# Decode attention with a gated MLP: the last weight rows on 24 and 25 lanes, the output sum in 160-column halves

## The chip, the cores and the metric

The kernel runs on one core of one Trainium2 chip. The metric is the device time of one execution in microseconds; lower is better. A profiled execution gives the trace that is read here. Times in the text count from the start of the profiled span.

## The reference

One token for each of 4 batch rows, width 640, all inputs and the output in bf16:

```python
xn = layernorm(x)                                  # [4, 1, 640], no scale or shift
# A: attention over a cache, 32 heads of 128, 4096 cached rows a head
q = (xn @ wq)                                      # [640, 4096], split in 32 heads
p = softmax(q . k_cache / sqrt(128))               # k_cache, v_cache [4, 32, 4096, 128]
A = (p . v_cache).reshape(4, 1, 4096) @ wo         # wo [4096, 640]
# B: gated MLP; the sequence is 1, so w_sp is [1, 1] and b_sp is [1]
z = gelu_tanh(xn @ w_in)                           # w_in [640, 1728]
z1, z2 = z[..., :864], layernorm(z[..., 864:])
B = (z1 * (w_sp * z2 + b_sp)) @ w_out              # w_out [864, 640]
out = x + A + B
```

K and V are 134 MB each; the weights w_q, w_o, w_in and w_out come to 13.8 MB.

## The kernel before

The work is cut into 16 units (`NU`), each with 8 heads of one batch row. A unit's K is 8 MB and its V is 8 MB. A load has 128 partitions with 64 KB in a row each. K lies in a ring of seven quarter slots (`k_ring`), V in one buffer (`v_all`).

For each quarter of a unit's K, `product` (L537, DVE) multiplies K by the broadcast query, `fold_half` (L543, DVE) adds the two halves of each row, and `sums` (L555, PE) adds the rest by matmuls with an identity into PSUM; `row_sums` (L569, DVE) ends the scores. `head_max`, `exps` and `by_head` make the softmax weights (ACT, DVE), `weighted` (L631, PE) multiplies them with V, and every four units `group_turn` and `group_proj` (L678 to L699) apply w_o. The output is summed in one PSUM tile, `out_ps`: partitions 0 to 3 hold the sum for columns 0 to 319, partitions 32 to 35 the one for columns 320 to 639 (`out_sum`). It starts with x, added by a matmul with the identity (L373).

All large loads are issued by SP's queue in the order of the list `loads`; `pump` issues the next one when its buffers are no longer in `busy`. The list starts with the first half of unit 0's K in two loads, then `load_w` (w_in, and w_out's first 768 rows), the second half of that K, `load_w_few` (w_out's last 96 rows) and unit 1's K; after these V and K alternate. w_q is loaded before all of them (L118). V's buffer holds w_q, w_in and w_out's first 640 rows at the start, so unit 0's V waits for the MLP's matmuls. The order of instructions on PE, DVE, ACT and SP is the order in which they are written in the `manual_schedule` block.

w_out's 864 rows are placed by `W_OUT`, with lanes, rows a lane and number of transfers: 128 x 5 in one, 128 x 1 in one, and 12 x 8 in four transfers of three lanes each (each lane then is one run of 8 rows, 10240 bytes).

```python
W_OUT = ((P, 5, 1), (P, 1, 1), (12, 8, 4))
```

The MLP is the generator `gmlp`; its steps run between the first two quarters of unit 0. w_sp and b_sp, 2 bytes each, are loaded by ACT after the first query has been copied (L735, L736). x is one transfer of four rows, issued by ACT (L101).

At the end `group_proj` adds the last eight heads, for each head columns 0 to 319 and then 320 to 639. w_o's last group comes in six transfers, the last head in two halves of 320 columns. ACT copies the whole of `out_ps` (L823), and ACT and SP write one half of the output each (L824, L825).

## Time and profile before

| what | value |
|---|---|
| time, median of 3 runs | 662.07 us (661.95 to 662.16) |
| time of the profiled execution | 662.09 us |
| its span, first to last instruction | 660.2 us |
| mean granted TensorE clock | 0.692 |
| busy: PE, DVE, ACT, POOL | 317.0, 522.6, 29.9, 10.1 us |
| moved by DMA | 282.55 MB, 428 GB/s over the span |
| share of 16 DMA engines' span on SP's and ACT's load queues | 99.1% and 0.0% |

The profiled execution's time is the span and 1.9 us outside it. Busy times of different engines overlap. The DMA share is the mean over the core's 16 DMA engines; a 128-row load gives each of them eight rows. "SPq" and "ACTq" are the issues of transfers on SP's and ACT's queue, not the transfers themselves.

### The profile page before, as it was taken

What the parts mean: (1) busy time and instruction counts of PE and PEld (TensorE: products, weight loads), DVE (VectorE), ACT (ScalarE), POOL (GpSimd) and SP (SyncE); (2) the same over time, 40 slices, a digit from 0 to 9 for tenths busy, and PEclk for the clock granted to TensorE, in tenths of its full rate; (3) what the DMA queues carried; (4) which work ended last, traced back from release to release, by engine and by line L of the source; (5) the groups of instructions that cost most, each with busy time, mean ns of one, the idle gap of its engine ahead of it and who ended that gap; (6) DMA issues with size and microseconds to landing.
All of it is one profiled execution on the core that took longest, in us unless ns stands there. A gap on an engine that the chain in (4) does not pass through costs nothing.

```text
span 660.2 us, 4777 instructions
## 1 busy us (share of the span) xinstructions
PE 317.0 (48%) x2083; PEld 136.3 (21%) x2083; DVE 522.6 (79%) x276; ACT 29.9 (5%) x73; POOL 10.1 (2%) x20
## 2 busy tenths in 40 slices
PE   0574372526427363452636336263452534737367
PEld 0231121212213121120212112121120211212124
DVE  1767978959597795969959598695969969999950
ACT  0020000000000000000000000000000000000000
POOL 2300000000000000000000000000000000000000
PEclk9757676766767676585767768676685867676785
DMA  9999999999999999999999999999999999999997
GB/s 369 433 461 434 417 441 434 433 437 438 421 445 426 437 430 441 437 422 433 434 441 441 418 437 441 430 441 421 434 441 437 426 421 445 422 427 436 449 409 284
DMA packets 8232, 282.55 MB, mean 428 GB/s; under 512 B 892, under 2 KB 2184, under 8 KB 2568
## 3 DMA queue, kind: packets, MB, share of 16 engines
q1 hardware_dynamic: 8192, 282.25, 99.1%
q8 instruction: 16, 0.26, 0.1%
q10 hardware_dynamic: 20, 0.01, 0.0%
q14 instruction: 4, 0.03, 0.0%
HBM read 282.24 MB, written 0.01 MB: 428 GB/s over the span
## 4 chain that ended last, share of the span: by engine, by line
DMA 62%; DVE 28%; PE 8%; issue 1%; ACT 0%; DVEq 0%
DMA k_ring<-in_A_k_cache_dram 53%; DVE k_ring L537 14%; DVE k_ring L543 7%; PE s_ps L555 6%; DMA v_all<-in_A_v_cache_dram 4%; DMA k_ring<-in_A_wo_dram 3%; DVE s_sb L569 3%; DMA v_all<-in_A_wq_dram 2%; DVE p_m L607 1%; DVE m L578 1%; PE q_ps L303 1%; PE pv L631 1%; PE out_ps L699 1%; DVE p_m L678 1%; DVE mf L580 1%
## 5 line engine op out<-in xcount | busy, mean ns | idle before, releaser
L537 DVE TENSOR_TENSOR k_ring<-k_ring,qbc 128x8192 bf16<-128x8192 bf16 x64 | 282.9, 4420 | 88.5 <-DMA k_ring<-in_A_k_cache_dram 87.9
L555 PE MATMUL s_ps<-k_ring,ident 128*128 128x512 bf16 x512 | 202.2, 566 | 313.8 <-DVE k_ring L543 313.7
L555 PEld LDWEIGHTS <-ident 128*128 128x128 bf16 x512 | 64.0, 130 | 430.0 <-issue 245.4
L543 DVE TENSOR_TENSOR k_ring<-k_ring 128x4096 bf16<-128x4096 bf16 x64 | 145.9, 2280 | 1.1
L631 PE MATMUL pv<-v_all,p_m 128*32 128x512 bf16 x960 | 62.5, 419 | 0.0
L569 DVE TENSOR_REDUCE s_sb<-s_ps 128x128 f32<-128x1024 f32 x32 | 39.0, 1218 | 3.7 <-PE s_ps L555 3.7
L607 DVE TENSOR_TENSOR p_m<-p_c,own 128x2048 bf16<-128x2048 bf16 x16 | 36.6, 2285 | 0.7 <-ACT p_c L596 0.7
L631 PEld LDWEIGHTS <-p_m 128*32 128x32 bf16 x992 | 26.6, 106 | 42.5 <-issue 23.3
L596 ACT ACTIVATE p_c<-s_sb,nm 128x256 bf16<-128x256 f32 x16 | 8.1, 508 | 342.9 <-DVE nm L588 342.9
L662 PEld LDWEIGHTS o_ps<-o_rows,pick 128*128 128x128 f32 x96 | 20.4, 294 | 4.3 <-issue 3.3
L662 PE MATMUL o_ps<-o_rows,pick 128*128 128x128 f32 x96 | 19.1, 367 | 0.0
L643 ACT COPY o_rows<-pv 128x512 f32<-128x512 f32 x16 | 9.4, 586 | 165.7 <-PE pv L631 165.7
L311 DVE TENSOR_SCALAR q_rows<-q_ps 128x512 bf16<-128x512 f32 x2 | 1.4, 692 | 12.8 <-PE q_ps L303 12.8
L817 DVE TENSOR_TENSOR o_n_last<-o_last,rden_all 128x32 bf16<-128x32 f32 x1 | 0.2, 192 | 12.2 <-PE o_last L809 12.2
L303 PE MATMUL q_ps<-v_all,xnT 128*32 128x512 bf16 x40 | 4.5, 630 | 9.3 <-DMA v_all<-in_A_wq_dram 9.3
L527 ACT CAST qbc<-qbc_ps 128x128 bf16<-128x128 f32 x16 | 4.3, 266 | 97.6 <-PE qbc_ps L519 97.6
L578 DVE TENSOR_REDUCE m<-s_sb 128x1 f32<-128x256 f32 x16 | 6.7, 420 | 0.5
L519 PE MATMUL qbc_ps<-q_rows,of_row 128*128 128x128 bf16 x32 | 6.0, 276 | 0.6 <-DVE q_rows L311 0.6
L519 PEld LDWEIGHTS <-of_row 128*128 128x128 bf16 x32 | 4.1, 132 | 8.1 <-issue 7.4
L716 PE MATMUL o_last<-hot,o_rows 128*128 128x8 f32 x32 | 4.9, 279 | 0.7 <-ACT o_rows L643 0.7
L716 PEld LDWEIGHTS o_last<-hot,o_rows 128*128 128x128 f32 x32 | 4.8, 226 | 1.8 <-ACT o_rows L643 1.6
L699 PE MATMUL out_ps<-k_ring,p_m 128*4 128x320 bf16 x48 | 4.0, 309 | 2.1 <-DVE p_m L691 2.1
(87 smaller groups left out, 81.4 us busy)
## 6 DMA issues: line engine op xcount, KB each, us to landing
k_ring<-in_A_k_cache_dram SPq DMA_DIRECT2D x5, 4096.0 KB, 27.2
v_all<-in_A_v_cache_dram SPq DMA_DIRECT2D x2, 4096.0 KB, 28.2
v_all<-in_A_wq_dram SPq DMA_DIRECT2D x1, 5120.0 KB, 15.4
k_ring<-in_A_k_cache_dram SPq DMA_DIRECT2D x2, 2048.0 KB
k_ring<-in_A_v_cache_dram SPq DMA_DIRECT2D x1, 4096.0 KB
k_ring<-in_A_wo_dram SPq DMA_DIRECT2D x3, 1280.0 KB, 20.6
v_all<-in_B_w_in_dram SPq DMA_DIRECT2D x1, 2160.0 KB
k_ring<-in_A_v_cache_dram SPq DMA_DIRECT2D x1, 2048.0 KB
```

What stands on the lines that cost most here:

```text
L303: nc.tensor.matmul(out=q_ps[k * QD : (k + 1) * QD], lhsT=xnT[:, c, :], rhs=wq_v[:, c, k, e], start=(c == 0), stop=(c == DC - 1),)
L519: nc.tensor.matmul(out=qb_ps[:], lhsT=of_row[:, e, b].rearrange("p k f l -> p (k f l)"), rhs=q_rows[e][:, hg, :], start=(e == 0), stop=(e ...
L537: nc.vector.tensor_tensor(out=t, in0=t, in1=qbcs[u][:, None, :].to_broadcast([P, HC, Dh]), op=ALU.mult)
L543: nc.vector.tensor_tensor(out=t[:, :, 0:HD2], in0=t[:, :, 0:HD2], in1=t[:, :, HD2:Dh], op=ALU.add)
L555: nc.tensor.matmul(out=s, lhsT=ident[:], rhs=t[:, :, g * RW : (g + 1) * RW], start=(g == 0), stop=(g == m - 1),)
L569: nc.vector.tensor_reduce(out=scores[u][:].rearrange("p (r c) -> p r c", r=NK)[:, lo : hi + 1 : hi - lo], in_=sums_ps.pop(n // 2)[:], axis ...
L578: nc.vector.tensor_reduce(out=m1[:], in_=scores[u][:], axis=AX.X, op=ALU.max)
L607: nc.vector.tensor_tensor(out=p_m[:, u % 2], in0=p_c.pop(u)[:].rearrange("p (g c) -> p g c", c=CB)[:, :, :, None].to_broadcast([P, NG, CB, HT]
L631: nc.tensor.matmul(out=pvs[u][cg * QD : (cg + 1) * QD, :], lhsT=p_m[:, u % 2, g0 + n].rearrange("p c h -> p (c h)"), rhs=v_at[:, n * CB : ...
L662: nc.tensor.matmul(out=gr[hg][:], lhsT=pick[:, c, Bsz - 1 - b : P + Bsz - 1 - b], rhs=o[:, c, :], start=(b == 0 and c == 0), stop=(b == Bs ...
L699: nc.tensor.matmul(out=out_sum(half), lhsT=o, rhs=wo_sb[:, n, half * NOH : (half + 1) * NOH], start=False, stop=(hg == HG - 1 and n == HT ...
L716: nc.tensor.matmul(out=o_last[0][:, :, :, u % Bsz], lhsT=o[:, c, :], rhs=hot[:, c, :].rearrange("p (k e) -> p k e", e=PAR), start=(c == 0) ...
```

## The change

- w_out's rows 640 to 863 are placed on 24 lanes with one row each and on 25 lanes with eight rows each. On the 25 lanes a lane's eight rows follow each other in w_out, one run of 10240 bytes. They are loaded in small transfers: before the second half of unit 0's K ("wide") three for the 24 lanes, one of five lanes and half of one lane; after it ("few") two of five lanes, three of three lanes and the other half of that lane.
- x is loaded in four transfers of one row. w_sp and b_sp are loaded right after it, at the start.
- The two sums in `out_ps` hold alternate blocks of 160 columns (0 to 159 with 320 to 479, and 160 to 319 with 480 to 639). In the last head the first blocks of both are added first, then the second blocks. The last copy is made in two halves of 160 columns, by DVE and ACT. Each output transfer has two pieces of 160 columns a row.
- In `gmlp`, the factors of GELU and layer norm are folded into fewer DVE instructions, the mean comes from a matmul with a column of 1/864, and b_sp is carried through the broadcast and added in the last step.

The diff, cut to its core:

```diff
@@ -59,14 +59,18 @@
     RW = 8
     QW = HC * Dh
     RING = 2 * NK - 1
-    W_OUT = ((P, 5, 1), (P, 1, 1), (12, 8, 4))
+    W_OUT = (
+        (P, 5, True, (("wide", 0, 128, 1),)),
+        (24, 1, True, (("wide", 0, 12, 1), ("wide", 12, 8, 1), ("wide", 20, 4, 1))),
+        (25, 8, True, (("wide", 1, 5, 4), ("few", 2, 5, 4), ("few", 7, 5, 4), ("few", 0, 3, 4), ("few", 3, 3, 9), ("few", 16, 3, 4), ("half", 22, 1, 1))),
+    )
...
@@ -98,7 +102,13 @@
 
     ring = places.tile([P, RING, QW], BF16, name="k_ring")
     x_bf = ring[0:Bsz, 1, 0:D]
-    nc.scalar.dma_start(out=x_bf, in_=A_x.flatten_outer_dims())
+    x_rows = A_x.flatten_outer_dims()
+    for b0, b1 in ((0, 1), (1, 2), (2, 3), (3, 4)):
+        nc.scalar.dma_start(out=x_bf[b0:b1], in_=x_rows[b0:b1])
+    wsp_bf = const.tile([1, 1], BF16)
+    bsp_bf = const.tile([1, 1], BF16)
+    nc.scalar.dma_start(out=wsp_bf[:], in_=B_w_sp[0:1, 0:1])
+    nc.scalar.dma_start(out=bsp_bf[:], in_=B_b_sp[0:1].rearrange("(a b) -> a b", a=1))
     v_all = places.tile([P, NK * QW], BF16, name="v_all")
 
     wq_sb = v_all[:, 0 : DC * HD].rearrange("p (c n) -> p c n", c=DC)
@@ -107,35 +117,42 @@
 
     at_v = up(DC * (HD + F))
     w_parts, f0, at_p = [], 0, 0
...
-    def load_part(part):
-        w, f0, n, r, t = part
-        rows = B_w_out[f0 : f0 + n * r].rearrange("(p k) n -> p k n", k=r)
-        for l in range(t):
-            nc.sync.dma_start(out=w[l:n:t], in_=rows[l:n:t])
+    def load_part(part, on):
+        w, f0, n, r, near, cuts = part
+        rows = B_w_out[f0 : f0 + n * r].rearrange(
+            "(p k) n -> p k n" if near else "(k p) n -> p k n", k=r
+        )
+        for kind, l, m, step in cuts:
+            if kind == on:
+                end = l + (m - 1) * step + 1
+                nc.sync.dma_start(out=w[l:end:step], in_=rows[l:end:step])
+            if kind == "half":
+                part_r = slice(0, r // 2) if on == "wide" else slice(r // 2, r)
+                nc.sync.dma_start(out=w[l : l + m, part_r], in_=rows[l : l + m, part_r])
 
     def load_w():
         nc.sync.dma_start(out=w_in_sb, in_=B_w_in.rearrange("(p c) n -> p c n", c=DC))
         for part in w_parts:
-            if part[4] == 1:
-                load_part(part)
+            load_part(part, "wide")
 
     def load_w_few():
         for part in w_parts:
-            if part[4] > 1:
-                load_part(part)
+            load_part(part, "few")
 
     w_rows = [
-        (w[:, i], f0 + i, n, r) for w, f0, n, r, _ in w_parts for i in range(r)
+        (w[:, i], f0 + i * (1 if near else n), n, r if near else 1)
+        for w, f0, n, r, near, _ in w_parts
+        for i in range(r)
     ]
 
     def run_of(cache, u):
@@ -251,6 +268,9 @@
     nc.gpsimd.memset(eps_tile[:], eps)
     ones_sq = const.tile([P, P], FP32)
     nc.gpsimd.memset(ones_sq[:], 1.0)
+
+    inv_fh = const.tile([P, 1], FP32)
+    nc.gpsimd.memset(inv_fh[:], 1.0 / float(Fh))
 
     NACC = 2
     row_den = [const.tile([P, Bsz], FP32, name=f"rd{n}") for n in range(NACC)]
...
@@ -366,14 +384,20 @@
     out_ps = ps_out.tile([P, NOH], FP32)
     OG = 32
 
-    def out_sum(half):
-        return out_ps[OG * half : OG * half + Bsz, :]
+    NS = 2
+    NP = NOH // NS
+
+    def out_sum(g):
+        return out_ps[OG * g : OG * g + Bsz, :].rearrange("b (s n) -> b s n", s=NS)
+
+    def columns(w, g):
+        return w.rearrange("p (s g n) -> p g s n", s=NS, n=NP)[:, g]
 
     for half in range(2):
         nc.tensor.matmul(
-            out=out_ps[OG * half : OG * half + OG, :],
+            out=out_ps[OG * half : OG * half + OG, :].rearrange("b (s n) -> b s n", s=NS),
             lhsT=ident[:Bsz, :OG],
-            rhs=x_bf[:, half * NOH : (half + 1) * NOH],
+            rhs=columns(x_bf, half),
             start=True,
             stop=False,
         )
@@ -384,11 +408,11 @@
     gm["gz"] = work.tile([P, 3, NFC, Bsz], FP32, name="gz")
     nc.gpsimd.memset(gm["zz"][:], 0.0)
     gm["st"] = work.tile([1, 5 * Bsz], FP32, name="st")
-    gm["ac"] = work.tile([1, 2 * Bsz], FP32, name="ac")
+    gm["ac"] = work.tile([1, 2 * Bsz + 1], FP32, name="ac")
     gm["yT"] = work.tile([P, NFC, Bsz], BF16, name="yT")
 
     by_lanes = []
...
@@ -411,29 +435,33 @@
         yield
         k0 = 0
         for n, ks in by_lanes:
-            nc.vector.tensor_copy(
-                out=zz[0:n, :, k0 : k0 + ks, :], in_=zT[0:n, :, k0 : k0 + ks, :]
+            nc.vector.tensor_scalar(
+                out=zz[0:n, :, k0 : k0 + ks, :],
+                in0=zT[0:n, :, k0 : k0 + ks, :],
+                scalar1=0.5,
+                scalar2=None,
+                op0=ALU.mult,
             )
             k0 += ks
-        nc.vector.tensor_tensor(out=gw[:], in0=zz[:], in1=zz[:], op=ALU.mult)
-        nc.vector.tensor_scalar(
-            out=gw[:], in0=gw[:], scalar1=0.044715, scalar2=1.0, op0=ALU.mult, op1=ALU.add
-        )
-        nc.vector.tensor_tensor(out=gw[:], in0=gw[:], in1=zz[:], op=ALU.mult)
+        nc.vector.scalar_tensor_tensor(
+            out=gw[:], in0=zz[:], scalar=4 * 0.044715, in1=zz[:], op0=ALU.mult, op1=ALU.mult
+        )
+        nc.vector.scalar_tensor_tensor(
+            out=gw[:], in0=gw[:], scalar=1.0, in1=zz[:], op0=ALU.add, op1=ALU.mult
+        )
         nc.scalar.activation(
-            out=gt[:], in_=gw[:], func=ACT.Tanh, scale=math.sqrt(2.0 / math.pi)
+            out=gt[:], in_=gw[:], func=ACT.Tanh, scale=2 * math.sqrt(2.0 / math.pi)
         )
         yield
-        nc.vector.tensor_scalar(
-            out=gt[:], in0=gt[:], scalar1=1.0, scalar2=0.5, op0=ALU.add, op1=ALU.mult
-        )
-        nc.vector.tensor_tensor(out=gz[:, 0:2], in0=zz[:], in1=gt[:], op=ALU.mult)
+        nc.vector.scalar_tensor_tensor(
+            out=gz[:, 0:2], in0=gt[:], scalar=1.0, in1=zz[:], op0=ALU.add, op1=ALU.mult
+        )
         sq = gz[:, 2, :, :]
         nc.vector.tensor_tensor(out=sq, in0=gz[:, 1, :, :], in1=gz[:, 1, :, :], op=ALU.mult)
 
         s_ps = ps_m.tile([1, 2, NFC, Bsz], FP32, tag="m", name="ln_ps")
         nc.tensor.matmul(
-            out=s_ps[:], lhsT=ones_sq[:, 0:1], rhs=gz[:, 1:3], start=True, stop=True
+            out=s_ps[:], lhsT=inv_fh[:], rhs=gz[:, 1:3], start=True, stop=True
         )
         yield
         st, ac = gm["st"], gm["ac"]
@@ -448,13 +476,6 @@
             axis=AX.X,
             op=ALU.add,
         )
-        nc.vector.tensor_scalar(
-            out=st[:, 0 : 2 * Bsz],
-            in0=st[:, 0 : 2 * Bsz],
-            scalar1=1.0 / float(Fh),
-            scalar2=None,
-            op0=ALU.mult,
-        )
         nc.vector.tensor_tensor(out=tmp_t, in0=mean_t, in1=mean_t, op=ALU.mult)
         nc.vector.tensor_tensor(out=var_t, in0=ex2_t, in1=tmp_t, op=ALU.subtract)
         nc.scalar.activation(
@@ -462,27 +483,25 @@
         )
         wsp_t = work.tile([1, 1], FP32, name="wsp_t")
         nc.gpsimd.tensor_copy(out=wsp_t[:], in_=wsp_bf[:])
-        bsp_t = work.tile([1, 1], FP32, name="bsp_t")
-        nc.gpsimd.tensor_copy(out=bsp_t[:], in_=bsp_bf[:])
+        nc.gpsimd.tensor_copy(out=ac[:, 2 * Bsz :], in_=bsp_bf[:])
         yield
         nc.vector.reciprocal(out=rst_t, in_=rst_t)
         nc.vector.tensor_scalar(
             out=ac[:, 0:Bsz], in0=rst_t, scalar1=wsp_t[:, 0:1], scalar2=None, op0=ALU.mult
         )
-        nc.vector.tensor_tensor(out=tmp_t, in0=ac[:, 0:Bsz], in1=mean_t, op=ALU.mult)
-        nc.vector.tensor_scalar(
+        nc.vector.scalar_tensor_tensor(
             out=ac[:, Bsz : 2 * Bsz],
-            in0=tmp_t,
-            scalar1=-1.0,
-            scalar2=bsp_t[:, 0:1],
+            in0=mean_t,
+            scalar=-1.0,
+            in1=ac[:, 0:Bsz],
             op0=ALU.mult,
-            op1=ALU.add,
-        )
-        ac_ps = ps_m.tile([P, 2 * Bsz], FP32, tag="m", name="ac_ps")
+            op1=ALU.mult,
+        )
+        ac_ps = ps_m.tile([P, 2 * Bsz + 1], FP32, tag="m", name="ac_ps")
         nc.tensor.matmul(
             out=ac_ps[:], lhsT=ones_sq[0:1, :], rhs=ac[:], start=True, stop=True
         )
-        ac_sb = work.tile([P, 2 * Bsz], FP32, name="ac_sb")
+        ac_sb = work.tile([P, 2 * Bsz + 1], FP32, name="ac_sb")
         nc.scalar.copy(out=ac_sb[:], in_=ac_ps[:])
         yield
         nc.vector.tensor_tensor(
@@ -497,13 +516,20 @@
             in1=ac_sb[:, None, Bsz : 2 * Bsz].to_broadcast([P, NFC, Bsz]),
             op=ALU.add,
         )
-        nc.vector.tensor_tensor(out=gm["yT"][:], in0=gz[:, 0, :, :], in1=sq, op=ALU.mult)
+        nc.vector.scalar_tensor_tensor(
+            out=gm["yT"][:],
+            in0=sq,
+            scalar=ac_sb[:, 2 * Bsz :],
+            in1=gz[:, 0, :, :],
+            op0=ALU.add,
+            op1=ALU.mult,
+        )
         for k, (w, _, n, _) in enumerate(w_rows):
             for half in range(2):
                 nc.tensor.matmul(
                     out=out_sum(half),
                     lhsT=gm["yT"][0:n, k, :],
-                    rhs=w[:, half * NOH : (half + 1) * NOH],
+                    rhs=columns(w, half),
                     start=False,
                     stop=False,
                 )
@@ -695,14 +721,17 @@
 
     def group_proj(hg):
         for n, o in enumerate(gr.pop(hg)):
-            for half in range(2):
-                nc.tensor.matmul(
-                    out=out_sum(half),
-                    lhsT=o,
-                    rhs=wo_sb[:, n, half * NOH : (half + 1) * NOH],
-                    start=False,
-                    stop=(hg == HG - 1 and n == HT - 1),
-                )
+            last = hg == HG - 1 and n == HT - 1
+            for s in range(NS) if last else [None]:
+                for half in range(2):
+                    y, w = out_sum(half), columns(wo_sb[:, n, :], half)
+                    nc.tensor.matmul(
+                        out=y if s is None else y[:, s],
+                        lhsT=o,
+                        rhs=w if s is None else w[:, s],
+                        start=False,
+                        stop=last and s == NS - 1,
+                    )
         busy.remove(WO_AT)
 
 
@@ -732,8 +761,6 @@
     E = mybir.EngineType
     with tc.manual_schedule(engines={E.PE, E.DVE, E.Activation, E.SP}):
         stage_q(0)
-        nc.scalar.dma_start(out=wsp_bf[:], in_=B_w_sp[0:1, 0:1])
-        nc.scalar.dma_start(out=bsp_bf[:], in_=B_b_sp[0:1].rearrange("(a b) -> a b", a=1))
         waiting = None
         mlp = gmlp()
         for n in range(NK * NU):
@@ -819,10 +846,15 @@
         group_proj(HG - 1)
 
         res = v_all[:, 0:NOH]
-        out_v = out.flatten_outer_dims()
-        nc.scalar.copy(out=res[0 : OG + Bsz], in_=out_ps[0 : OG + Bsz])
-        nc.scalar.dma_start(out=out_v[:, 0:NOH], in_=res[0:Bsz])
-        nc.sync.dma_start(out=out_v[:, NOH:D], in_=res[OG : OG + Bsz])
+        rows = slice(0, OG + Bsz)
+        nc.vector.tensor_copy(out=res[rows, 0:NP], in_=out_ps[rows, 0:NP])
+        nc.scalar.copy(out=res[rows, NP:NOH], in_=out_ps[rows, NP:NOH])
+        out_v = out.flatten_outer_dims().rearrange("b (s g n) -> b g s n", s=NS, n=NP)
+        for g, dma in enumerate((nc.scalar, nc.sync)):
+            dma.dma_start(
+                out=out_v[:, g],
+                in_=res[OG * g : OG * g + Bsz].rearrange("b (s n) -> b s n", s=NS),
+            )
 
 
 # ---- launch: one core; inputs and outputs as the reference has them ----
```

More of the change, by code (lines that the diff above doesn't have):

```diff
@@ L61 @@
     RING = 2 * NK - 1
-    W_OUT = ((P, 5, 1), (P, 1, 1), (12, 8, 4))
-    assert sum(n * r for n, r, _ in W_OUT) == Fh
-    NFC = sum(r for _, r, _ in W_OUT)
+    W_OUT = (
[3 more added lines that the diff above has]
+    )
+    assert sum(n * r for n, r, _, _ in W_OUT) == Fh
+    NFC = sum(r for _, r, _, _ in W_OUT)
     def up(n):
         return -(-n // 256) * 256
-    PW = sum(up(r * D) for _, r, _ in W_OUT[1:])
+    PW = sum(up(r * D) for _, r, _, _ in W_OUT[1:])
     NOH = D // 2
@@ L109 @@
     w_parts, f0, at_p = [], 0, 0
-    for n, r, t in W_OUT:
+    for n, r, near, cuts in W_OUT:
         if f0 == 0:
@@ L115 @@
             at_p += up(r * D)
-        w_parts.append((room.rearrange("p (k n) -> p k n", k=r), f0, n, r, t))
+        w_parts.append((room.rearrange("p (k n) -> p k n", k=r), f0, n, r, near, cuts))
         f0 += n * r
     nc.sync.dma_start(out=wq_sb, in_=A_wq.rearrange("(p c) n -> p c n", c=DC))
-    def load_part(part):
-        w, f0, n, r, t = part
-        rows = B_w_out[f0 : f0 + n * r].rearrange("(p k) n -> p k n", k=r)
-        for l in range(t):
-            nc.sync.dma_start(out=w[l:n:t], in_=rows[l:n:t])
+    def load_part(part, on):
[10 more added lines that the diff above has]
+                nc.sync.dma_start(out=w[l : l + m, part_r], in_=rows[l : l + m, part_r])
     def load_w():
@@ L281 @@
     )
-    wsp_bf = const.tile([1, 1], BF16)
-    bsp_bf = const.tile([1, 1], BF16)
     xn_v = xn_bf.rearrange("b (p c) -> b c p", c=DC)
@@ L386 @@
     gm["st"] = work.tile([1, 5 * Bsz], FP32, name="st")
-    gm["ac"] = work.tile([1, 2 * Bsz], FP32, name="ac")
+    gm["ac"] = work.tile([1, 2 * Bsz + 1], FP32, name="ac")
     gm["yT"] = work.tile([P, NFC, Bsz], BF16, name="yT")
     by_lanes = []
-    for n, r, _ in W_OUT:
+    for n, r, _, _ in W_OUT:
         if by_lanes and by_lanes[-1][0] == n:
```

## The prediction

> **What bounds the kernel now.** I read the page first, then the chain of waits, then the last four microseconds in small windows, then the first microseconds in order of time, and last the packet records of the trace (start, length, size and queue of every packet).
>
> ```profile
> PE 317.0 (48%) x2083; PEld 136.3 (21%) x2083; DVE 522.6 (79%) x276; ACT 29.9 (5%) x73; POOL 10.1 (2%) x20
> ...
> DMA  9999999999999999999999999999999999999997
> ...
> q1 hardware_dynamic: 8192, 282.25, 99.1%
> q8 instruction: 16, 0.26, 0.1%
> ```
>
> No compute engine is full; the DMA engines are, in every slice but the last. The queue that carries the loads is busy for 99.1% of 16 engines' span. Work on DVE, ACT, POOL or PE counts only where it stops a load from being queued, or after the last load. The chain of waits ends so:
>
> ```profile
> 634.09 21.98 DMA k_ring<-in_A_wo_dram
> 656.11 1.29 PE out_ps L699 x8
> ```
>
> So the end is the landing of w_o's last piece, then eight matmuls (the last one starts at 656.96 by its record), ACT's copy and the two output transfers. How evenly the sixteen DMA engines reach that end stands in the windows view (the last two columns are DMA share and GB/s):
>
> ```profile
> 653.60:654.00 0.40, 0.40 (x15) 0.40 (x16) 0.00 (x0) 0.00 (x0) 0.00 (x0) 0.50 1.01 366
> 654.00:654.40 0.40, 0.20 (x8) 0.10 (x4) 0.17 (x1) 0.00 (x0) 0.00 (x0) 0.50 0.89 322
> 654.40:654.80 0.40, 0.32 (x4) 0.19 (x5) 0.02 (x1) 0.00 (x0) 0.00 (x0) 0.50 0.90 307
> 654.80:655.20 0.40, 0.38 (x4) 0.03 (x1) 0.00 (x0) 0.00 (x0) 0.00 (x0) 0.50 0.66 235
> 655.20:655.60 0.40, 0.31 (x4) 0.17 (x4) 0.00 (x0) 0.00 (x0) 0.00 (x0) 0.50 0.55 187
> 655.60:656.00 0.40, 0.39 (x4) 0.04 (x1) 0.00 (x0) 0.00 (x0) 0.00 (x0) 0.50 0.53 160
> 656.00:656.40 0.40, 0.29 (x4) 0.15 (x4) 0.00 (x0) 0.00 (x0) 0.00 (x0) 0.50 0.25 75
> 656.40:656.80 0.40, 0.40 (x6) 0.32 (x4) 0.00 (x0) 0.00 (x0) 0.00 (x0) 0.50 0.04 11
> ```
>
> From 654.0 the engines run out one after another, the last (by the records) at 656.63. Idle share times 0.4 us is 0.4 x 3.18 = 1.27 us up to 656.8, so 1.1 us up to 656.63: with sixteen equal engines the last load would land 1.1 us earlier. That is all the loads can give.
>
> The packet records say who is late. Each 128-row load ends with sixteen completion writes of 4 bytes, one per DMA engine, and their distances from the first are the same from load to load within a few ns. They change only by instruction packets: when one of the 16 packets of q8 (16 KB, 0.88 to 0.97 us) passes, one engine falls back by 1.42 us. This goes round over eight engines, so each of them loses 2.84 us. An 8 KB instruction packet costs its engine 0.55 to 0.84 us; four came, on three others. At 630.5 us the distances were 0, 0.47, 0.76, 0.95, 1.40, 1.47, 1.53, 1.54, 1.72, 2.02, 2.57, 2.59, 2.68, 2.78, 2.86 and 3.20 us. The six from 2.57 up have had both instruction packets; 1.40 and 1.47 each get one more and come to about 2.85. The three that take w_out's 12 lanes stand at 1.53, 1.72 and 2.02 (this one had an 8 KB packet): the four three-row transfers all used the same three engines, one 10240-byte packet each, 0.387 us apart. The end is set by 3.20, an engine that also began wq 0.63 us late against 0 to 0.32 for the seven like it.
>
> **The change part by part.**
>
> *w_out's last rows.* Before, the 128-lane part gave every engine 8 packets of 1280 bytes (0.42 us, 52.4 ns each), and the 12 lanes gave three engines 4 x 0.387 = 1.55 us more: 1.97. Taking the x load (four rows, four engines) and the three-row loads as the pattern, a transfer of n < 16 lanes goes to the same first n engines, a lane each. The new pieces are single rows for 12, 8 and 4 lanes (0.058 each with a completion write of 6 ns), 10240-byte lanes by three transfers of 5 and three of 3, and one lane in two pieces of 5120 bytes (0.20 each, half of 0.387, on the first engine). First engine: 3 x 0.058 + 6 x 0.387 + 0.40 = 2.90, so +0.93. Second and third: 2.50, +0.53. Fourth: 3 x 0.058 + 3 x 0.387 = 1.34, +0.92. Fifth: 1.28, +0.86. The others have 2, 1 or 0 rows, so -0.30 to -0.42. The latest engine goes from 3.20 to about 2.80. w_sp and b_sp show the first engine: it is the one at 1.72, and goes to 2.65; the other two go to 2.06 and 2.55. So the last landing moves by -0.40; if the late starter is not late again, the others are at 2.49 and the first engine decides, -0.55. I take -0.40. Ends: -1.1 (full balance) and +0.5 (second rival).
>
> *Last head, copy, output.* At the granted clock of 0.50 matmuls of 512 columns follow each other 0.427 us apart (s_ps at 600.86, 601.29, 601.72), 0.83 ns a column. After the last landing half 1 runs 320 columns; afterwards both groups of 160 run side by side, as the pairs of L699 do now (records 2 ns apart): -0.13. ACT's copy took 0.420 for 320 columns; by its rows of 128 (0.266) and 512 columns (0.586) 160 cost 0.29: -0.13. DVE's half, between its PSUM rows of 48 columns (0.165) and 512 (0.692), is about 0.29, and its columns are complete earlier; even if it waits for the last matmul it ends with ACT's. Each output row is two pieces of 320 bytes and not one of 640; the 640-byte packets took 0.03, so +0.03, and one more semaphore wait lies beside the copy. Sum -0.23; ends -0.30 and +0.1.
>
> [...]
>
> *x in four rows, w_sp and b_sp early.* ACT issues six DMAs at the start and not one (0.23 to 0.56 us each). SP's wq is its first instruction still. On one engine, small transfers take turns with the loads' packets:
>
> ```profile
> 21.66 0.23 ACTq L735 DMA_DIRECT2D wsp_bf<-in_B_w_sp_dram  x1
> 21.92 0.46 ACTq L736 DMA_DIRECT2D bsp_bf<-in_B_b_sp_dram  x1
> ...
> 26.98 1.76 POOL L464 CAST wsp_t<-wsp_bf 1x1 f32<-1x1 bf16 x1 [21.53 <-DMA wsp_bf<-in_B_w_sp_dram]
> 28.69 4.39 POOL L466 CAST bsp_t<-bsp_bf 1x1 f32<-1x1 bf16 x1
> ```
>
> Two bytes took 5 us; their data and completion writes came one 17280-byte packet (0.65 us) apart. If a single row goes to the first engine, the six packets of x's last three rows stand between wq's of 1.51 us: x lands near 2.1 + 2.3 + 9.1 = 13.5 us and not at 3.0. xnT needs 4.2 more (3.01 to 7.18), so q starts at 17.7 instead of 16.15. Cover: k1's load, released by the first PE sums and issued at 32.04, is wanted only when the first K load's second half is through (41.4, less 1.1 from issue to first packet). The cover is 8.3 us; cost nothing.
>
> *Six more SP transfers.* There are eight completion semaphores in turn, so each transfer waits for the eighth before it. K0's second half then waits for K0's second quarter, as w_out's second small piece did (by about 25.7 us); queued behind it are w_out's rest and k1. The engines have w_in and w_out until 31.7 us: nothing. k1 waits for a small piece (near 33) and goes out near 35, again before 40.3.
>
> *GELU and layer-norm steps, b_sp last, the 1/Fh column.* Some four DVE steps of 0.15 to 0.22 us fewer, one copy of 0.17 more, at 36 to 45 us, and DVE then waits for K (4.03 us before 63.06): nothing. Nor do strided moving columns of the same count.
>
> **Sum.** 662.09 (profiled; span 660.2 plus 1.9 outside; the median is 662.07) - 0.40 - 0.23 = 661.46, so 661.5. Its own range is 661.0 to 661.9. About 0.2%, or 1.32 us, is what a measurement of this kernel can tell from no change: this forecast lies within it.
>
> **Rivals.**
> *The engines come out level* (0.30). If the five filled engines get no instruction packet, the late starter is gone, and the early turns on the first engine cost nothing, most of the 1.1 us comes: 662.09 - 1.1 - 0.26 = 660.7, faster by just over 0.2%. For it: 2.90 us of rows on the first engine are what two instruction packets cost, 2.84. Against it: three of the engines that are not hit (now 0 to 0.95) get hardly any rows, so some slack stays.
> *A filled engine is also hit* (0.10). The records don't number the engines. If the fourth or fifth is one of the eight, it goes from 2.8 to 3.7, 0.5 past today's end: 662.09 + 0.5 - 0.23 = 662.4, within 0.2%.
> *x comes too late* (0.12), the one on the slower side. Place: the first engine's queue. It decides once x lands after 11.95 + 8.3 = 20.2 us: every us beyond delays k1 past the end of its cover, and all sixteen engines stand idle. If the rows get through only behind K0's first half (24.5 us), the price is 4.3 us: 665.8. For it: two bytes took 5 us behind smaller packets. Against it: taking turns gives 13.5. [...]
>
> **Numbers.** Forecast 0.48 and hit engine 0.10 are within 0.2%: 0.58. Level engines: 0.30 faster. Late x: 0.12 slower. The range 660.4 to 662.9 leaves out the late x and the far ends.
>
> **What would show it.** The DMA share of the last windows falls from 1 to 0 within about 2.5 us and not 2.9; between the last landing and ACT's end lie 1.0 us and not 1.2; q_ps starts at 16 to 18 us; no slice before the last has less than 9 tenths of DMA. Wrong: q_ps after 24, a gap in the DMA row near 41 us, one engine alone at the end for over 0.5 us, or output transfers landing 0.3 us later after their issue than now.

## The result: slower by 0.26%

| | before | after |
|---|---|---|
| median of 10 runs each | 662.01 us (661.79 to 662.19) | 663.67 us (663.59 to 663.83) |
| ratio | | 1.0026, 95% interval 1.0018 to 1.0033 |
| span of the profiled execution | 660.22 us | 661.76 us |
| last landing of w_o, by the packet records | 656.63 | 657.31 |
| from there to the end of the span | 3.59 | 4.45 |

The forecast was 661.5 us, within 0.2% of before. The time is 663.67, slower by more than that and above the range's 662.9. The two terms of the sum came out with the other sign: the loads end 0.68 us later and not 0.40 earlier, and what follows them takes 0.86 us more and not 0.23 less. Together these are the spans' 1.54 us. (Of the seven runs of the kernel own25 below, three took 670 to 686 us, for a reason that stays open; its readings rest on the other four, but two of the three are in its ratio.)

**What bounds it** has not changed. The page of after:

```profile
PE 315.2 (48%) x2085; PEld 136.6 (21%) x2085; DVE 522.2 (79%) x274; ACT 29.7 (4%) x73; POOL 4.3 (1%) x21
...
DMA  9999999999999999999999999999999999999996
...
q1 hardware_dynamic: 8128, 282.25, 99.0%
q8 instruction: 16, 0.26, 0.1%
```

The DMA engines are full to the last slice, with the same bytes. The chain of waits of after ends so (start, us, what):

```profile
634.42 22.34 DMA k_ring<-in_A_wo_dram
656.77 0.04 issue
656.81 1.25 PE out_ps L728 x10
658.08 0.33 DVE v_all L850
658.43 0.29 ACT v_all L851
```

Where it read w_o, eight matmuls and one copy, there are now two copies, one behind the other. The windows view of after (DMA share and GB/s in the last two columns):

```profile
654.00:654.40 0.40, 0.00 (x1) 0.01 (x1) 0.00 (x0) 0.00 (x0) 0.00 (x0) 0.50 1.00 355
654.40:654.80 0.40, 0.40 (x15) 0.40 (x16) 0.00 (x0) 0.00 (x0) 0.00 (x0) 0.50 0.81 301
...
655.60:656.00 0.40, 0.38 (x6) 0.04 (x4) 0.00 (x0) 0.00 (x0) 0.00 (x0) 0.50 0.84 286
656.00:656.40 0.40, 0.40 (x4) 0.21 (x4) 0.00 (x0) 0.00 (x0) 0.00 (x0) 0.50 0.71 235
656.40:656.80 0.40, 0.29 (x4) 0.00 (x0) 0.00 (x0) 0.00 (x0) 0.00 (x0) 0.50 0.42 131
656.80:657.20 0.40, 0.39 (x4) 0.21 (x4) 0.00 (x0) 0.00 (x0) 0.00 (x0) 0.50 0.09 29
```

Three engines are through early (0.84 is about 13.4 of 16), most of the others run out between 656.0 and 656.8, and all of it lies later than before, when the share had fallen to 0.66 at 654.8.

**Where the loads lost it.** The mean of the sixteen completion writes of the load near 631 us is 632.34 before and 633.01 after: +0.67. At unit 1's K (61 us) it is 61.56 and 62.17: +0.61. So nearly the whole loss is there by 61 us, and the 570 us that follow add 0.06. It arises in packets that start at 40 to 46 us. There, in after, 26 packets of K of 65536 bytes take 2.46 to 3.61 us (all but two of them at most 3.06) where they took 2.42, on all sixteen engines, beside the last small pieces of w_out. Their excess is 10.0 us of engine time, that is, summed over the engines; with 0.8 us on five of the small pieces themselves it is 10.8, and 10.8 / 16 = 0.67. In before it is 0. (The records do not number the engines, but the packets of one engine follow each other without a gap, so an engine can be followed from packet to packet.) A coarser sign stands in the windows view from 20 to 60 us, before and then after: 441 and 434 GB/s.

```profile
20.00:60.00 40.00, 21.72 (x211) 10.55 (x204) 32.26 (x29) 5.14 (x8) 6.10 (x2) 0.64 1.03 441
```

```profile
20.00:60.00 40.00, 23.21 (x228) 12.37 (x221) 29.62 (x26) 5.14 (x8) 0.00 (x0) 0.67 1.03 434
```

Seven GB/s over 40 us are 0.28 MB, at 434 GB/s 0.65 us. The engines are "busy" all the time (1.03 in both): a stretched packet counts as work.

**Where the end lost it.** Timeline of after (start, us, queue or engine, line; what it waited for in brackets):

```profile
658.08 0.32 DVE L850 CAST v_all<-out_ps 36x160 bf16<-36x160 f32 x1 [2.85 <-PE out_ps L728]
658.43 0.29 ACT L851 CAST v_all<-out_ps 36x160 bf16<-36x160 f32 x1 [9.62 <-DVE v_all L850]
658.74 0.80 SPq L854 DMA_DIRECT2D out_dram<-v_all  x1
658.75 0.74 ACTq L854 DMA_DIRECT2D out_dram<-v_all  x1
```

and of before:

```profile
657.43 0.42 ACT L823 CAST v_all<-out_ps 36x320 bf16<-36x320 f32 x1 [9.36 <-PE out_ps L699]
657.87 0.30 SPq L825 DMA_DIRECT2D out_dram<-v_all  x1
657.88 0.28 ACTq L824 DMA_DIRECT2D out_dram<-v_all  x1
```

ACT's half names DVE's half as what it waited for: 0.66 us to the issue and not 0.44, +0.22. The issue of one output transfer takes 0.80 and 0.74 us and not 0.30 and 0.28, and from issue to the last output's landing it is 1.86 us and not 0.98, +0.88. By the packet records each row's two pieces of 160 columns were carried as single pieces of 320 bytes, eight a transfer. The matmuls took 0.03 less, and the wait after the output 0.21 less. 0.22 + 0.88 - 0.03 - 0.21 = 0.86.

### The profile page after: what moved, and what is told of

Same layout as the page of the kernel before. It is cut to its first block, busy times and chain, and to the rows that moved or that the text cites. A ratio compares the mean times of both kernels' runs of the same rounds, so it can differ in the third digit from the quotient of the medians.

```text
span 661.8 us, 4797 instructions
## 1 busy us (share of the span) xinstructions
PE 315.2 (48%) x2085; PEld 136.6 (21%) x2085; DVE 522.2 (79%) x274; ACT 29.7 (4%) x73; POOL 4.3 (1%) x21
## 4 chain that ended last, share of the span: by engine, by line
DMA 64%; DVE 27%; PE 7%; issue 1%; SPq 1%; DVEq 0%; ACT 0%
DMA k_ring<-in_A_k_cache_dram 52%; DVE k_ring L563 13%; DVE k_ring L569 6%; PE s_ps L581 6%; DMA v_all<-in_A_v_cache_dram 4%; DMA k_ring<-in_A_wo_dram 3%; DVE s_sb L595 3%; DMA v_all<-in_B_w_out_dram 2%; DMA v_all<-in_A_wq_dram 2%; DVE p_m L633 1%; DVE m L604 1%; DVE p_m L704 1%; PE out_ps L728 1%; PE pv L657 1%; DVE mf L606 1%
## 5 line engine op out<-in xcount | busy, mean ns | idle before, releaser
L428 PE MATMUL zT<-xnT,v_all 128*25 128x4 bf16 (+2 forms) x140 | 6.4, 183 | 0.0
L428 PEld LDWEIGHTS <-v_all 128*25 128x25 bf16 (+2 forms) x140 | 6.3, 134 | 0.0
L728 PE MATMUL out_ps<-k_ring,p_m 128*4 128x320 bf16 x48 | 4.4, 333 | 2.2 <-DVE p_m L717 2.2
```

What stands on the lines that cost most here:

```text
L428: nc.tensor.matmul(out=zT[0:n, t, k, :], lhsT=w_t[:, c, f : f + (n - 1) * r + 1 : r], rhs=xnT[:, c, 0:Bsz], start=(c == 0), stop=(c == DC ...
L728: nc.tensor.matmul(out=y if s is None else y[:, s], lhsT=o, rhs=w if s is None else w[:, s], start=False, stop=last and s == NS - 1,)
```

## The experiments

All were timed in five rounds beside the kernel before (its median then was 661.91 to 661.97 us). "Landing" is w_o's last landing in the profiled execution, "mean" the mean completion near 631 us.

### The change taken apart

**tail_undone**: after, with the sum, the copy and the output of before.

```diff
-        nc.vector.tensor_copy(out=res[rows, 0:NP], in_=out_ps[rows, 0:NP])
-        nc.scalar.copy(out=res[rows, NP:NOH], in_=out_ps[rows, NP:NOH])
...
+        nc.scalar.copy(out=res[0 : OG + Bsz], in_=out_ps[0 : OG + Bsz])
+        nc.scalar.dma_start(out=out_v[:, 0:NOH], in_=res[0:Bsz])
+        nc.sync.dma_start(out=out_v[:, NOH:D], in_=res[OG : OG + Bsz])
...
```

> The changed kernel with the end of before: output sums in halves of 320 adjacent columns, the last head in two matmuls, one copy by ACT, two output transfers of 640-byte rows. The changed profile has 4.45 us from the last w_o landing to the end of the span against 3.59 before. Theory 1 (half of the loss lies behind the last landing: copies one after the other and slow output transfers): 0.86 us faster than the changed kernel, about 662.8, and the slow stretch of loads near 44 us stays. Rival (all of the loss is in the loads, and the end only waits for them): as the changed kernel, 663.7.

Measured: 662.85 us, ratio 1.0013 (1.0004 to 1.0022), and the stretched packets stay. The changed end costs 663.67 - 662.85 = 0.82 us.

**lanes_undone**: after, with w_out's last rows placed as before.

```diff
-        (24, 1, True, (("wide", 0, 12, 1), ("wide", 12, 8, 1), ("wide", 20, 4, 1))),
-        (25, 8, True, (("wide", 1, 5, 4), ("few", 2, 5, 4), ("few", 7, 5, 4), ("few", 0, 3, 4), ("few", 3, 3, 9), ("few", 16, 3, 4), ("half", 22, 1, 1))),
+        (P, 1, True, (("wide", 0, 128, 1),)),
+        (12, 8, True, tuple(("few", l, 3, 4) for l in range(4))),
```

> The changed kernel with w_out's last rows as before: 128 lanes of one row, and 12 lanes by four transfers of three lanes, each lane four from the next. In the changed profile all K packets that are under way from 43.4 to 45.6 us take up to 0.63 us longer than 2.42, while the pieces on 25 lanes are loaded; the sixteen engines are 0.67 us later in the mean from there to the end. Theory 1 (the new pieces slow all engines): no slow packets, last landing 0.6 to 1.0 earlier, about 662.9. Rival (the slow stretch comes from x landing late, which moves the MLP to 40 to 48 us): the slow packets stay, 663.4 to 663.7.

Measured: 662.87 us, ratio 1.0013 (1.0004 to 1.0022). Mean 632.31, no stretched packets at 40 to 46 us, landing 656.36. The placement costs 663.67 - 662.87 = 0.80 us. The two parts add up: 663.67 - 0.82 - 0.80 = 662.05, the time of before.

**x_undone**: after, with x in one transfer, and w_sp and b_sp loaded where they were.

```diff
-    for b0, b1 in ((0, 1), (1, 2), (2, 3), (3, 4)):
-        nc.scalar.dma_start(out=x_bf[b0:b1], in_=x_rows[b0:b1])
+    nc.scalar.dma_start(out=x_bf, in_=A_x.flatten_outer_dims())
...
-    nc.scalar.dma_start(out=wsp_bf[:], in_=B_w_sp[0:1, 0:1])
...
         stage_q(0)
+        nc.scalar.dma_start(out=wsp_bf[:], in_=B_w_sp[0:1, 0:1])
...
```

> The changed kernel with x as one transfer of four rows and w_sp and b_sp after the first query, as before. Theory 1 (the late x is covered, the pieces on 25 lanes slow the engines): q starts at 16.2 again, the slow packets stay near 42 to 46 us, time 663.5 to 663.8. Rival (the late x and the MLP at 40 to 48 us cause the slow stretch): no slow packets, about 663.0.

Measured: 663.99 us, ratio 1.0030 (1.0019 to 1.0042). That is 0.32 us more than after, and above what was expected. The stretched packets stay (13.9 us of engine time), so x's single rows do not cause them. **x_four** is the converse, before with x's four rows and the early w_sp and b_sp, the same lines put in:

> The kernel of before with x in four one-row transfers and w_sp and b_sp right behind it. Theory (the late x is covered): x lands near 14 us, q starts near 18.3, unit 1's K is issued near 34 to 36 us, no gap in the loads, 661.8 to 662.2. Rival (the first DMA engine, or the late start, costs): 0.3 us or more slower.

Measured: 662.31 us, ratio 1.0006 (0.9997 to 1.0014). x lands at 13.94 us, and k1 still goes out at 34.24, before it is needed:

```profile
13.94 0.87 DVE L271 BATCH_NORM_STATS2 stats<-k_ring 4x6 f32<-4x320 bf16 x2 [13.94 <-DMA k_ring<-in_A_x_dram]
...
34.24 0.35 SPq L170 DMA_DIRECT2D k_ring<-in_A_k_cache_dram  x1
```

Its landing is 656.67, within 0.04 us of before. Its time is 0.38 us longer, as much as the rival asked for; the interval leaves open whether that is real, and x_undone, where taking x's change out made after slower, points the other way.

**mlp_only**: before with the changed arithmetic of the MLP alone.

```diff
-        nc.vector.tensor_tensor(out=gw[:], in0=zz[:], in1=zz[:], op=ALU.mult)
...
+        nc.vector.scalar_tensor_tensor(
+            out=gw[:], in0=zz[:], scalar=4 * 0.044715, in1=zz[:], op0=ALU.mult, op1=ALU.mult
+        )
...
```

> The kernel of before with the changed MLP arithmetic alone (folded factors, column of 1/864, b_sp added in the last step). All of it lies beside the loads: 661.8 to 662.1. Rival (fewer DVE steps bring something): under 661.7.

Measured: 662.01 us, ratio 1.0001 (0.9992 to 1.0009). It costs nothing.

### Which lanes a small transfer takes

In before, each three-lane transfer takes lanes four apart. **adjacent_lanes** is before with neighbouring lanes:

```diff
-            nc.sync.dma_start(out=w[l:n:t], in_=rows[l:n:t])
+            m = n // t
+            nc.sync.dma_start(out=w[l * m : (l + 1) * m], in_=rows[l * m : (l + 1) * m])
```

> The kernel of before with one edit: each of the four transfers of w_out's 12 last lanes takes three adjacent lanes and not three that are four apart. Same bytes, packets, engines and queue places. Theory 1a (a piece is slow, and slows others, when its engine writes lanes that another engine serves in the 128-lane loads): slow packets appear near 42 us, 0.1 to 0.7 us slower, 662.1 to 662.7. Theory 1b (only the number or the order of small transfers matters): no difference, 662.0.

Measured: 662.00 us, ratio 1.0001 (0.9992 to 1.0010): no change of time. But packets were stretched, by 2.7 us of engine time at 42 to 44 us, where before has none, and the mean moved to 632.54, +0.20. In the profiled execution the last engine stood 2.63 us behind the first and not 3.20, and the landing was 656.42. The sign was there, too small to decide, so the next pair makes it large.

**own25** and **adjacent25**: after, with the 25 lanes in four transfers of 7, 6, 6 and 6 lanes, in both kernels at the same places in the queue, of the same sizes and from the same engines. In own25 the lanes of a transfer lie four apart, in adjacent25 side by side.

```diff
own25, against after
+        (25, 8, True, (("wide", 1, 6, 4), ("few", 0, 7, 4), ("few", 2, 6, 4), ("few", 3, 6, 4))),
adjacent25, against after
+        (25, 8, True, (("wide", 7, 6, 1), ("few", 0, 7, 1), ("few", 13, 6, 1), ("few", 19, 6, 1))),
```

> The changed kernel with the 25 lanes in four transfers whose lanes are four apart (lanes 1, 5, ... ; 0, 4, ...; 2, 6, ...; 3, 7, ...), the first before the second half of unit 0's K and three after. Engine j then writes only lanes 4j to 4j + 3, which it also serves in a 128-lane load if that gives each engine lanes in fours. Engines one to six get 4 lanes each, the seventh gets one. Theory 1 (writing lanes that belong to another engine slows all of them): no slow packets at 40 to 47 us (under 1.5 engine-us in excess, the changed kernel has 10.8), mean completion at 631 us as in lanes_undone, time 662.6 to 663.2. Rival (many lane packets while K's packets run, wherever they go): slow packets as in the changed kernel, 663.5 or more.

> As own25 in number, size and engines of the pieces (four transfers, 7, 6, 6 and 6 lanes), but each takes adjacent lanes (0 to 6, 7 to 12, 13 to 18, 19 to 24), so that several engines write the lanes of one. Theory 1: slow packets again, 0.4 to 1.0 us slower than own25, 663.3 to 664. Rival: the same as own25 within 0.2 us.

Measured: own25 663.85 us (median of four runs at 663.75 to 663.96; ratio 1.0067, 1.0027 to 1.0107), adjacent25 666.21 us, ratio 1.0067 (1.0054 to 1.0080), far above the 663.3 to 664 expected. Between the two lie 2.36 us, and the kernels differ in nothing but the choice of lanes. The chain's last load, own25 and then adjacent25:

```profile
634.90 21.98 DMA k_ring<-in_A_wo_dram
656.92 1.25 PE out_ps L728 x10
```

```profile
637.14 21.97 DMA k_ring<-in_A_wo_dram
659.16 1.25 PE out_ps L728 x10
```

The whole end is shifted by 2.24 us; from w_o's landing to the end of the span it is only 0.08 longer. The stretch from 20 to 60 us moves 443 GB/s in own25 and 409 in adjacent25:

```profile
20.00:60.00 40.00, 24.18 (x224) 12.72 (x217) 30.17 (x27) 5.14 (x8) 0.00 (x0) 0.57 1.03 443
```

```profile
20.00:60.00 40.00, 23.35 (x228) 12.31 (x221) 29.79 (x26) 5.14 (x8) 0.00 (x0) 0.62 1.01 409
```

The records number neither the engines nor the lanes. The long pieces fall on the engines as if the i-th lane of a small transfer, counted from 0, always went to the same engine (six engines with four and one with one in own25; 8, 6, 6, 3 and 3 in after). In every transfer of long lanes of before and own25 the i-th lane is one of lanes 4i to 4i + 3; such a lane is called in place here, any other out of place. (The expectations call a lane in place its engine's own. That it is the same engine's in other loads was the author's assumption; no run shows it.) Counted so, the kernels sort:

| kernel | 10240-byte lanes | of them out of place | stretched packets, us of engine time | mean |
|---|---|---|---|---|
| before | 12 | 0 | 0 | 632.34 |
| adjacent_lanes | 12 | 6 | 2.7 | 632.54 |
| own25 | 25 | 0 | 0 | 632.48 |
| after | 25 | 11 | 10.8 | 633.01 |
| adjacent25 | 25 | 22 | 36.5 | 634.68 |

(For adjacent25 8.0 at 30 to 33 us, beside the transfer that goes early, and 28.5 at 40 to 46.) The mean moves by a sixteenth of the excess, within 0.1 us: by 0.20 for 0.17 (adjacent_lanes) and 0.67 for 0.67 (after), both from before, and 2.20 for 2.28 (adjacent25, from own25). So in these five kernels the long pieces cost their own bytes where they are in place, and more where they are not: a piece of 0.387 us that is out of place stretches packets by 0.45 us of engine time in adjacent_lanes, 1.0 in after and 1.7 in adjacent25, in the last two on all sixteen engines. The amount is not fixed: the same 11 lanes gave 13.9 us in x_undone and about 16 in tail_undone (1.8 of it at 30 to 33 us). That the choice of lanes makes the loss is shown by the pair. That it is their place in the transfer rests on this sorting; lanes side by side in one transfer are not needed, since after has none among its long lanes. What happens in the chip when lanes are out of place is not shown.

own25 was expected near 663 and missed for another reason. Its engines keep their pace, and one of them is overfilled: at 631 us the distances from the first are 3.28 us for the second latest and 4.23 for the latest. This one, followed through the records, carries four long lanes and also took the 16 KB instruction packets at 93.5 and 470.5 us. The windows view of own25:

```profile
656.00:656.40 0.40, 0.34 (x4) 0.20 (x4) 0.00 (x0) 0.00 (x0) 0.00 (x0) 0.50 0.35 110
656.40:656.80 0.40, 0.36 (x4) 0.02 (x1) 0.00 (x0) 0.00 (x0) 0.00 (x0) 0.50 0.08 27
656.80:657.20 0.40, 0.28 (x4) 0.15 (x4) 0.00 (x0) 0.00 (x0) 0.00 (x0) 0.50 0.07 21
```

0.07 is one engine of sixteen, alone for 0.9 us up to the landing at 657.41.

**own20** is before with 64 lanes of one row and 20 lanes of eight rows in four transfers of lanes four apart, and the changed MLP.

```diff
+        (64, 1, True, (("wide", 0, 64, 1),)),
+        (20, 8, True, (("wide", 0, 5, 4), ("few", 1, 5, 4), ("few", 2, 5, 4), ("few", 3, 5, 4))),
```

> A version drawn from the runs: before's x and end, the changed MLP arithmetic, and w_out's last 224 rows on 64 lanes of one row (one transfer, 4 packets an engine) and 20 lanes of eight rows (four transfers of five lanes that are four apart, so that engines one to five write their own lanes, four each). The engines with instruction packets lose 4 packets of 52 ns, the fourth and fifth gain 1.34 us, no packets are slowed. Theory: last landing 0.1 to 0.3 us earlier than before, 661.6 to 661.9. Rival (the fourth or fifth engine becomes the last): 662 or more.

Measured: 662.02 us, ratio 1.0004 (0.9995 to 1.0013); landing 656.47, 0.16 earlier than before. Other packets were stretched by 3.0 us of engine time at 30 to 33 us, where the 64 rows and five long lanes in place are loaded; 3.0 / 16 takes back 0.19. What stretched them is not shown: the table counts long lanes alone, and at the same place tail_undone, with 24 single rows, has 1.8, after 0.2 and own25 none. The time is the rival's 662 and not the 661.6 to 661.9 expected. No version was measurably faster than before.

### The end taken apart

**out_pieces**: before, with the sums in alternate blocks and so two pieces of 320 bytes a row in each output transfer; ACT's single copy stays.

```diff
-        nc.scalar.dma_start(out=out_v[:, 0:NOH], in_=res[0:Bsz])
-        nc.sync.dma_start(out=out_v[:, NOH:D], in_=res[OG : OG + Bsz])
+        out_v = out_v.rearrange("b (s g n) -> b g s n", s=NS, n=NP)
+        for g, dma in enumerate((nc.scalar, nc.sync)):
+            dma.dma_start(out=out_v[:, g], in_=res[OG * g : OG * g + Bsz].rearrange("b (s n) -> b s n", s=NS))
```

> The kernel of before with the two sums in alternate blocks of 160 columns, and so with output transfers of two 320-byte pieces a row; one copy by ACT, the last head in two matmuls as before. Theory 2 (the pattern of the output transfers is slow): issue 0.74 to 0.80 us and not 0.28 to 0.30, last output landing 1.86 us after issue and not 0.98, of which 0.2 are given back in SP's last waits: 0.6 to 0.7 us slower than before, 662.6. Rival (the two copies in turn are the loss, small pieces are free): 662.0.

Measured: 662.73 us, ratio 1.0012 (1.0003 to 1.0021), +0.82. Its timeline:

```profile
657.50 0.42 ACT L829 CAST v_all<-out_ps 36x320 bf16<-36x320 f32 x1 [9.68 <-PE out_ps L705]
657.95 0.78 SPq L832 DMA_DIRECT2D out_dram<-v_all  x1
657.95 0.75 ACTq L832 DMA_DIRECT2D out_dram<-v_all  x1
```

The issue is as long as in after, and the last output lands 1.88 us after its start. **out_four** writes the same 320-byte pieces from before's layout, by two plain transfers on each queue:

```diff
+        for s in range(2):
+            c = slice(s * NP, (s + 1) * NP)
+            nc.scalar.dma_start(out=out_v[:, s * NP : (s + 1) * NP], in_=res[0:Bsz, c])
+            nc.sync.dma_start(out=out_v[:, NOH + s * NP : NOH + (s + 1) * NP], in_=res[OG : OG + Bsz, c])
```

> The kernel of before with the output written by four transfers of 4 rows by 320 bytes, two on each queue, and not two of 640 bytes. [...] Reason a (the two-level pattern of two pieces a row): each transfer is issued in 0.28 to 0.30 us, the second of a queue lands about 0.3 us after the first, 0.2 to 0.4 us slower than before, 662.2. [...]

Measured: 662.26 us, ratio 1.0005 (0.9996 to 1.0014). The two issues together take less than the one above, and the last output lands 1.24 us after the first issue:

```profile
657.70 0.65 SPq L828 DMA_DIRECT2D out_dram<-v_all  x2
657.70 0.62 ACTq L827 DMA_DIRECT2D out_dram<-v_all  x2
```

So it is mainly the two-level pattern of one transfer that costs, not the size of its pieces: the 320-byte packets took 18 to 20 ns and the 640-byte ones 29 to 34.

**two_copies**: before, with the last copy by DVE and ACT in two halves of 160 columns.

```diff
-        nc.scalar.copy(out=res[0 : OG + Bsz], in_=out_ps[0 : OG + Bsz])
+        nc.vector.tensor_copy(out=res[0 : OG + Bsz, 0:NP], in_=out_ps[0 : OG + Bsz, 0:NP])
+        nc.scalar.copy(out=res[0 : OG + Bsz, NP:NOH], in_=out_ps[0 : OG + Bsz, NP:NOH])
```

> The kernel of before with the last copy in two halves of 160 columns, DVE and then ACT, and output transfers as before. Theory 2: ACT's half waits for DVE's, 0.32 + 0.03 + 0.29 against 0.42, so 0.2 us slower, 662.15. Rival (in the changed kernel something else held ACT; here both run side by side): 0.1 us faster, 661.85.

Measured: 662.34 us, ratio 1.0006 (0.9997 to 1.0015). In the trace the halves stand one behind the other as in after, with 0.66 us from the first copy's start to the issue and not 0.44:

```profile
657.47 0.32 DVE L824 CAST v_all<-out_ps 36x160 bf16<-36x160 f32 x1 [3.00 <-PE out_ps L699]
657.82 0.29 ACT L825 CAST v_all<-out_ps 36x160 bf16<-36x160 f32 x1 [10.47 <-DVE v_all L824]
658.13 0.30 SPq L827 DMA_DIRECT2D out_dram<-v_all  x1
```

Two things are shared by the halves: the tile that they write and the one that they read. **copies_two_tiles** gives them two to write, and sends the output in four transfers as out_four does, ACT's half first.

```diff
+        res_b = work.tile([P, NP], BF16, name="res_b")
-        nc.scalar.copy(out=res[0 : OG + Bsz, NP:NOH], in_=out_ps[0 : OG + Bsz, NP:NOH])
+        nc.scalar.copy(out=res_b[0 : OG + Bsz], in_=out_ps[0 : OG + Bsz, NP:NOH])
```

> The kernel before, with the last copy in two halves of 160 columns by DVE and ACT that go to two different result tiles, and the output in four transfers of 160 columns each (ACT's half is sent first on both queues). Theory one: ACT waited for DVE because both halves were written to one tile; then ACT's copy starts within 0.05 us of DVE's, both are through about 0.33 us after the last matmul and not 0.66, and the time is that of the output in four transfers less 0.1: about 662.15 us. Theory two: the order comes from the sum's tile, which both read; then ACT starts again after DVE's end, 0.35 us later, and the time is about 0.2 above that of the output in four transfers: 662.45 us.

Measured: 662.79 us, ratio 1.0013 (1.0004 to 1.0022); above both expectations. Its trace decides between them:

```profile
657.32 0.32 DVE L825 CAST v_all<-out_ps 36x160 bf16<-36x160 f32 x1 [3.03 <-PE out_ps L699]
657.67 0.29 ACT L826 CAST res_b<-out_ps 36x160 bf16<-36x160 f32 x1 [9.90 <-DVE v_all L825]
```

ACT still starts when DVE is through, so the tile that they write is not the reason. What is left is that both read `out_ps`. Whether a sum in two tiles would let them run together was not tried, and whether the wait lies in the program or in the chip is not shown. The 0.82 us above before are about what two_copies (0.43) and out_four (0.33) cost together.

The parts of the end do not add up as those of the whole change do: out_pieces costs 0.82 us and two_copies 0.43, but the whole end 0.82 in tail_undone. From landing to the end of the span the traces have +0.91, +0.26 and, for after, +0.86. The new order of the last head was not run alone, so where after wins this back is open.

## Why the prediction was wrong

**w_out's last rows (-0.40, measured +0.68).** This is the first step that failed. It priced each packet by its own length on its own engine and let the transfers go to "the same first n engines, a lane each", whichever lanes those were. The packet lengths were right for long pieces in place (own25: none stretched). What it left out is that 11 of the 25 long lanes are out of place, and that packets on all sixteen engines were stretched, by 10.8 us of engine time in all: +0.67 on the mean. The trace of before could not show it, since all its 12 lanes are in place.

Nor did the balance come. The step let the latest engine go from 3.20 to 2.80 us behind the first. At 631 us it stood at 3.15, which is 1.07 us behind the mean where before had 1.41. Then the instruction packet at 641.5 us came: in the next completion writes the engine at 2.09 stands at 3.50, 1.41 further back, and is the last (3.50 is 1.42 behind the mean of 631 us). It is not the rival of a filled engine that is also hit: followed back through the records, this engine carries no long lane, and it had taken the packet at 287.3 us, eight packets earlier. None of after's five filled engines took a 16 KB packet. What the step had missed is that an engine that is not filled can be the last: in before the two that still had a packet to come stood at 1.40 and 1.47 us and came to about 2.85, while this one stood at 2.09. Why it stood so late is open; already at 61 us it was the latest of the engines neither filled nor hit. So even without the stretching the landing would have stayed where it was: +0.67 and +0.01 make the 0.68.

**Last head, copy, output (-0.23, bounds -0.30 to +0.1, measured +0.86).** This is the second. The matmuls were to give 0.13 and gave 0.03. The copies were to give 0.13 and cost 0.22, because ACT's half waits for DVE's; the text weighed only a wait for the last matmul. The two pieces a row were to cost 0.03, by the packets' lengths, and cost 0.88, of which 0.50 is the longer issue itself and the rest lies between its end and the landing: the trace of before has no transfer with two pieces a row to a DRAM output, and the bound was set by the wrong quantity, the packet and not its description. Of what the prediction named as a sign of error, "output transfers landing 0.3 us later after their issue than now" came true, three times over.

**What held.** x queued on one engine and landed at 14.15 us (forecast 13.5), q started at 18.32 (17.7), K0's second half went out at 25.52 (25.7) and k1 at 36.00 (35), before 40.3, so nothing waited:

```profile
0.74 1.38 ACTq L107 DMA_DIRECT2D k_ring<-in_A_x_dram  x4
14.15 0.88 DVE L285 BATCH_NORM_STATS2 stats<-k_ring 4x6 f32<-4x320 bf16 x2 [14.15 <-DMA k_ring<-in_A_x_dram]
18.32 4.46 PE L321 MATMUL q_ps<-v_all,xnT 128*32 128x512 bf16 x40 [0.33 <-DVE xnT L312]
25.52 0.35 SPq L181 DMA_DIRECT2D k_ring<-in_A_k_cache_dram  x1
36.00 0.36 SPq L181 DMA_DIRECT2D k_ring<-in_A_k_cache_dram  x1
```

The rival of the late x is refuted by this and by x_undone. A row of x was one packet of 1280 bytes on one engine, 53 to 55 ns long, and the four started at 1.67, 5.97, 9.05 and 12.13 us. The turn of eight semaphores shows in SP's waits in after: w_in waited 13.5 us for wq, the eighth transfer before it, and K0's second half 4.6 us for K0's second quarter. The MLP's steps cost nothing, as mlp_only shows, nor did the strided columns: `group_proj`'s 48 matmuls of 320 columns before the last group take 299 ns (median) in before (L699) and in after (L728). And the bound on what the loads could give at best, 1.1 us, was right to make this a change of small gains: the two terms missed by as much as that bound (1.08 and 1.09). The rival of level engines takes the end at -0.26, without its 0.03 for the pieces; with the sum's -0.23 it gives 660.8 and not 660.7.

## What to carry to other kernels

Where the DMA engines are full, try the lanes of a small transfer four apart and beginning with one of the first four (own25 had no stretched packets, adjacent25 with its lanes side by side 36.5 us of them), and judge a placement by the lengths of the *other* transfers' packets, since a stretched packet counts as busy (the DMA share from 20 to 60 us is 1.03 in before and in after). Price a transfer by its issue as well as by its packets: here one more level in the access pattern cost 0.82 us, more than the whole step was to bring. And where work is split over two engines at the very end, look in the trace for which of the two waits for the other before counting it as halved.

## What the runs showed of the hardware

- Small transfers of long rows to lanes side by side cost 2.36 us of the kernel's time against the same rows on lanes four apart (adjacent25, own25), and packets of all sixteen engines are stretched, from 2.42 us to as much as 4.11. By the sorting above, 22 of the 25 lanes are out of place there and none in own25.
- An output transfer of four rows with two 320-byte pieces each takes 0.74 to 0.80 us to issue, against 0.28 to 0.30 with one piece of 640; two plain transfers of 320 bytes a row take 0.62 to 0.65 together.
- DVE and ACT, copying different columns of one PSUM tile, ran one after the other, with 0.03 us between them, whether they wrote to one tile or to two.
- An instruction packet at 641.5 us, 16 us before the last landing, put its engine back by 1.41 us and so chose which engine is last in after; the same engine had taken the one at 287.3 us, eight packets earlier.
